# A list scheduler with clocks sets the order of attention and z1 on one Trainium2 core

## The chip, the core and the metric

The kernel runs on one core of a Trainium2 chip. The core has five engines with a queue each, which work through their queues in order: TensorE (PE, matmuls), VectorE (DVE), ScalarE (ACT), GpSimd (POOL) and SyncE (SP, which issues most DMAs). Matmul results land in PSUM, eight banks of 2 KB per partition. The metric is the device time of one execution in microseconds; the kernel before takes 1897.5 us (median of three runs, 1896.04 to 1898.21).

## What is computed

The input x is 2048 tokens of 576 features. With xn = layernorm(x), the reference computes, cut to what matters:

```
qkv = xn @ wqkv                                # 32 heads of 18
scores = q k^T * 18**-0.5, kept where 0 <= query - key < 256
s = softmax(scores) @ v @ wo
z = gelu(x @ w_in);  z1, z2 = z[:, :2304], layernorm(z[:, 2304:])
g = w_sp @ z2 + b_sp                           # w_sp is 2048 x 2048
out = x + s * silu((z1 * g) @ w_out)
```

The softmax subtracts each row's maximum, so scores are computed twice: once to find the maxima (rows are queries), once, transposed, for the exponential.

## The kernel before

Matrix products of the projections run with operands split in a high and a low half (fp32r), three matmuls for one. The stages stand one after the other: q and k projection (to 145 us), v, the z2 half of the gelu (204 to 442 us), **attention together with z1** (to 915 us), the product with w_sp by seven half-size products (to about 1600 us), and the output products.

In z2 and z1, PE is used as two row groups: contraction rows 0 to 63 and 64 to 127 hold different weights, and matmuls of the two groups run side by side. Class `RowGroups` hands out the matmuls of a 512-token tile: `lower()` issues the next one of the lower group (L288), `upper()` of the upper (L306). A tile has 13 or 14 on each side. A tile's upper side may start only when the lower side is through, which a one-element copy on VectorE (`turn`, L291) marks; then the tile is copied out by ScalarE (`evict`, L536). z1 has 72 tiles in three PSUM banks (pool `mmp`); its 972 matmuls per group are the filler for attention.

Attention handles 16 units: four heads, half of the queries. Head j of a unit lies in the lower row group for even j and in the upper for odd j. Per unit there are:

- 32 **row maxima** (`row_max`): a matmul of 256 or 384 columns into a bank of pool `sps` (L585 in the lower group, L589 in the upper, output `sp`), reduced by VectorE into `mx` (L478). After 32 of them `mx` is spread out, transposed in two matmuls (L490), split in two pieces by VectorE (L494, L495) and put beside q by four GpSimd DMAs (`put_max`, L498), so that the score matmul itself subtracts the maximum. One unit makes 35 items of a generator: 32 maxima, the spread, a pause, and both transposes.
- 32 or 40 **scores** (`scores`): a matmul into a bank of pool `tps` (also L585 or L589, output `tps`) and an exponential by ScalarE into `pt` (L627). Blocks on the edge of the band are masked by GpSimd (L630, L633).
- **PV** (`pv`): fp32 matmuls of all 128 rows by 32 columns per head (L647), whose result ScalarE copies out (L657) and SP stores.

The order is that of the program text, since the scheduler of the framework is switched off here. `beside` sets each score or maximum next to one z1 matmul of the other row group. In the main loop each score is followed by up to `FILL` = 2 pairs of z1 matmuls, as many as the shares `WEIGHT` allow, and up to three maxima at the rate `RMN` = 35 per unit, `FIRST` = 53 ahead. PV comes in bursts when three (unit, key block) entries are ready. `clock` is a rough time that only delays stores and puts (`after`, `tick`). Each of `sps` and `tps` has two banks, used in turn, and `ops` one. In z2, 53 items of the stream of maxima are issued in the last 26 tiles, two a tile, beside z2's matmuls.

Of the kernel before, what the change touches and what calls it, by code (L numbers as in the profile page):

```python
# [10 lines left out]
F32 = mybir.dt.float32  # L11
# [29 lines left out]
RMN = 35  # L41
LEAD = 18
FIRST = RMN + LEAD
SUMS_AT = 112
NPT = 6
FILL = 2
LAG = 8
ZORDER = [8 * (i // 8) + i % 2 * 4 + i % 8 // 2 for i in range(16)]
NORM_AT = 2
GAP = 7  # L50
# [3 lines left out]
TAIL = 56  # L54
HEAD = 14
_SHARE = [18 + 0.4 * (i >= 8) for i in range(16)]
WEIGHT = [sum(_SHARE[:i + 1]) / sum(_SHARE) for i in range(16)]

# [11 lines left out]
def kernel(  # L70
# [181 lines left out]
    with ExitStack() as early:  # L252
# [15 lines left out]
        class RowGroups:  # L268

            def __init__(self, tiles):  # L270
                self.tiles, self.n, self.i = tiles, -1, 0
                self.low, self.up, self.ready, self.hooks = [], [], [], {}

            def lower(self):
                if self.i == len(self.low):
# [7 lines left out]
                    if self.n < 2:  # L283
                        hook()
                    else:
                        self.hooks[self.n] = hook
# [3 lines left out]
                if self.i == len(self.low):  # L290
                    dve.tensor_copy(turn, self.last[3][0:1, 0:1])  # L291
                    self.ready.append(self.last)
                return True
# [5 lines left out]
            def upper(self):  # L299
                if not self.up:  # L300
                    if not self.ready or not (self.over or self.n > self.ready[0][0] and self.i >= LAG):
                        return False
                    self.up = self.ready.pop(0)
                    self.up = [self.up[0], self.up[1], self.up[2]]
                m, up, done = self.up
                up.pop(0)()  # L306
                if not up:
                    self.up = []
                    done()
                    if m + 2 in self.hooks:  # L310
                        self.hooks.pop(m + 2)()
                return True

# [101 lines left out]
        with ExitStack() as ph:  # L415
# [45 lines left out]
            def row_max(u):  # L461
                g, half = UNITS[u]
                base = 0 if half == 0 else 6
                mx = aa.tile([P, 2, 2, 4, 8], F32, name="mx")
                for a in range(2):
                    for i in range(8):
                        qb = 8 * half + i
                        w = 384 if qb >= 2 else 256
                        k0 = (max(qb - 2, 0) - base) * P
                        m0 = {0: 256, 1: 128}.get(qb, 0)  # L470
                        for b in range(2):
                            j = 2 * a + b
                            ps = sps.tile([P, 384], F32, name="sp")
                            mm = partial(pe.matmul, ps[:, :w], q_of(u, j, DR)[:, i * P:(i + 1) * P],
                                         k_of(u, j, DR)[:, k0:k0 + w], start=True, stop=True)
                            beside((mm, None) if b == 0 else (None, mm))
                            junk = aa.tile([P, 384], mybir.dt.bfloat16, name="junk")
                            dve.tensor_tensor_reduce(out=junk[:, :w], in0=ps[:, :w], in1=band[:, m0:m0 + w],  # L478
                                                     scale=1.0, scalar=-3.0e38, op0=ALU.add, op1=ALU.max,
                                                     accum_out=mx[:, a, b, 0, i:i + 1])  # L480
                            yield
                dve.tensor_copy(mx[:, :, :, 1:], mx[:, :, :, 0:1].to_broadcast([P, 2, 2, 3, 8]))
                yield
                yield
                hi = aa.tile([P, P], F32R, name="mh")
                m = aa.tile([P, P], F32R, name="mhl")
                pts_ = [sps.tile([P, 384], F32, name="sp")[:, :64] for _ in range(2)]
                for n in range(2):
# [833 lines left out]
```

## Time and profile before

| | before |
|---|---|
| median of three runs | 1897.5 us |
| profiled execution, its time | 1899.3 us |
| profiled execution, its span | 1897.6 us |
| PE busy | 1861.4 us (98%) |
| VectorE busy | 1075.8 us (57%) |
| ScalarE busy | 885.9 us (47%) |
| GpSimd busy | 297.7 us (16%) |
| granted TensorE clock | 0.999 |
| stage of z2 | 204 to 442 us |
| stage of attention and z1 | 438 to 915 us |

The span runs from the first instruction to the last; the execution's time has a little around it. Busy time is the union of an engine's records, so PE counts as busy when one of the two row groups is. A record of a matmul covers its whole latency; how often matmuls follow each other has to be read from starts.

### The profile page before, as it was taken

Reading aid. Unit: us, or ns where it says so; the run is one execution under the profiler, and the core shown is the slowest. Engines: PE = TensorE matmul, PEld = TensorE weight load, DVE = VectorE, ACT = ScalarE, POOL = GpSimd, SP = SyncE. Lnnn points to the kernel's source line nnn. Section 1 sums busy time; section 2 is a strip of 40 time slices with the busy share of each in tenths; the row PEclk is TensorE's granted clock in tenths of the full one; section 3 lists DMA queues with packets and bytes.
Section 4 is the critical chain, followed back from the end, with each engine's and each line's share of the span. In section 5 each row is a group of like instructions: output and inputs, shape, how many; then the busy total and the mean of one; then the engine's idle time right before and its main releaser. Section 6 shows DMA issues by size and latency. Waiting matters only on the chain.

```text
span 1897.6 us, 35556 instructions
## 1 busy us (share of the span) xinstructions
PE 1861.4 (98%) x13296; PEld 1584.7 (84%) x13296; DVE 1075.8 (57%) x2496; ACT 885.9 (47%) x1663; POOL 297.7 (16%) x419
## 2 busy tenths in 40 slices
PE   6999999999999999999999999999999999999998
PEld 5889999997677767666888888888888888999998
DVE  6521233367677776662386767676776877533222
ACT  3222222225666666667565565545655454432221
POOL 1002243343433443434000000000000000000000
PEclk9999999999999999999999999999999999999999
DMA  7664589964565665554676686757868578855442
GB/s 229 185 167 137 181 277 277 298 234 132 142 149 144 156 157 143 142 130 133 230 241 203 219 290 216 232 165 254 274 222 304 189 261 264 296 167 162 137 140 67
DMA packets 221383, 376.98 MB, mean 199 GB/s; under 512 B 41306, under 2 KB 118234, under 8 KB 221082
## 3 DMA queue, kind: packets, MB, share of 16 engines
q1 hardware_dynamic: 216378, 367.49, 62.7%
q10 hardware_dynamic: 2304, 5.09, 0.7%
q0 software_dynamic: 2528, 2.13, 0.4%
q8 instruction: 105, 1.72, 0.4%
q14 instruction: 68, 0.56, 0.1%
HBM read 256.52 MB, written 117.55 MB: 197 GB/s over the span
## 4 chain that ended last, share of the span: by engine, by line
PE 90%; DMA 5%; ACT 2%; DVE 2%; issue 1%; SPq 1%; POOL 0%; ACTq 0%; POOLq 0%
PE acc L1095 36%; PE po L1245 12%; PE mm L288 12%; PE mm L306 8%; PE mm L391 6%; PE ops L647 4%; PE vps L548 3%; PE tps L585 3%; PE sp L585 2%; PE wops L1199 2%; DMA s_d<-so 1%; PE sp L589 1%; DMA z_d<-zt 1%; PE tps L589 1%; ACT pt L627 1%
## 5 line engine op out<-in xcount | busy, mean ns | idle before, releaser
L1095 PE MATMUL acc<-sph,zh 128*128 128x512 f32 x1008 | 392.4, 389 | 0.2 <-DVE u L1068 0.2
L1095 PE MATMUL acc<-sph,zl 128*128 128x512 f32 x1008 | 392.3, 389 | 0.0
L1095 PE MATMUL acc<-spl,zh 128*128 128x512 f32 x1008 | 392.2, 389 | 0.0
L478 DVE CUSTOM_DVE_ANT_0 junk<-sp,band 128x384 bf16<-128x384 f32 (+1 forms) x512 | 265.6, 537 | 101.3 <-PE sp L585 32.9
L627 ACT ACTIVATE pt<-tps 128x384 f32<-128x384 f32 (+2 forms) x576 | 241.0, 439 | 107.3 <-PE tps L585 56.5
L306 PE MATMUL mm<-b,z1wh 64*128 64x512 f32 x648 | 237.7, 413 | 0.7 <-DVE turn L291 0.7
L235 DVE TENSOR_TENSOR spl<-spr,sph 128x1024 fp32r<-128x1024 f32 x166 | 203.2, 1224 | 50.2 <-ACT sph L235 47.0
L288 PE MATMUL mm<-b,z1wh 64*128 64x512 f32 x648 | 224.0, 395 | 0.0
L1095 PEld LDWEIGHTS acc<-sph,zh 128*128 128x128 f32 x1008 | 189.3, 188 | 40.0 <-issue 0.9
L1095 PEld LDWEIGHTS acc<-spl,zh 128*128 128x128 f32 x1008 | 189.3, 188 | 39.3
L1095 PEld LDWEIGHTS acc<-sph,zl 128*128 128x128 f32 x1008 | 189.3, 188 | 39.3
L235 ACT ACTIVATE zh<-b 128x384 fp32r<-128x384 f32 x144 | 75.6, 525 | 244.3 <-PE acc L1095 244.0
L288 PE MATMUL mm<-z2wh,b 64*128 64x384 f32 x720 | 185.5, 333 | 2.6 <-ACT zt L805 2.6
L306 PE MATMUL mm<-z2wh,b 64*128 64x384 f32 x720 | 183.6, 333 | 0.4 <-DVE turn L291 0.4
L235 ACT ACTIVATE sph<-spr 128x1024 fp32r<-128x1024 f32 x166 | 174.0, 1048 | 3.8 <-DMA spr<-in_w_sp_dram 2.7
L1245 PE MATMUL po<-b,yh 128*128 128x288 f32 x896 | 157.3, 296 | 0.5 <-ACT gs L1259 0.5
L235 DVE TENSOR_TENSOR zl<-b,zh 128x384 fp32r<-128x384 f32 x144 | 80.1, 557 | 116.0 <-ACT zh L235 115.8
L306 PE MATMUL mm<-b,z1wl 64*128 64x512 f32 x324 | 133.5, 412 | 0.0
L1245 PEld LDWEIGHTS po<-b,yh 128*128 128x128 f32 x896 | 132.7, 189 | 0.7 <-ACT gs L1259 0.7
L288 PEld LDWEIGHTS mm<-z2wh,b 64*128 64x128 f32 x720 | 128.4, 184 | 3.6 <-ACT zt L805 3.4
L805 ACT ACTIVATE zt<-mm 128x384 f32<-128x384 f32 x96 | 47.2, 491 | 176.3 <-PE mm L306 99.2
L306 PEld LDWEIGHTS mm<-z2wh,b 64*128 64x128 f32 x720 | 128.6, 184 | 1.0 <-DVE turn L291 1.0
(172 smaller groups left out, 3925.5 us busy)
## 6 DMA issues: line engine op xcount, KB each, us to landing
spr<-sc_d SPq DMA_DIRECT2D x96, 512.0 KB
spr<-in_w_sp_dram SPq DMA_DIRECT2D x72, 512.0 KB
zr<-z_d SPq DMA_DIRECT2D x136, 192.0 KB
st_d<-qkhl SPq DMA_DIRECT2D x72, 256.0 KB
z_d<-zt SPq DMA_DIRECT2D x96, 192.0 KB
z_d<-z1o SPq DMA_DIRECT2D x72, 256.0 KB
z1t<-z_d SPq DMA_DIRECT2D x72, 256.0 KB
yr<-y_d SPq DMA_DIRECT2D x48, 384.0 KB
```

The costliest lines, as they stand in the source:

```text
L235: job()
L288: self.low[self.i]()
L306: up.pop(0)()
L391: pe.matmul(ps, w, r, start=n == 0, stop=n == len(pl) - 1)
L478: dve.tensor_tensor_reduce(out=junk[:, :w], in0=ps[:, :w], in1=band[:, m0:m0 + w], scale=1.0, scalar=-3.0e38, op0=ALU.add, op1=ALU.max, ac ...
L548: pe.matmul(ps[:, i, :288], r, w[:, i * 288:(i + 1) * 288], start=n == 0, stop=n == len(pl) - 1)
L585: pair[0]()
L627: act.activation(pt[:, j, d0:d0 + n * P], ps[:, (qa - a) * P:(qa - a + n) * P], AF.Exp, scale=scale)
L647: pe.matmul(o_ps[c][32 * j:32 * j + 32, (lo - 4 * c) * P:(hi - 4 * c + 1) * P], vgs[u][:, kb - k0, j * VW:j * VW + 32], pt[:, j, (lo - kb) ...
L805: act.activation(zv, ps[:, :ZW], AF.Gelu_apprx_tanh)
L1095: pe.matmul(acc[j], z[:, ps], w[:, cs], start=s == i == 0 and n in OPENS, stop=s == 7 and i == 2, skip_group_check=True)
L1245: pe.matmul(po[i][:, a, :288], y[:, i * P:(i + 1) * P], w[:, a * 288:(a + 1) * 288], start=f == 0 and m == 0, stop=f == NF - 1 and m == 2)
```

## The change

`beside`, the shares and `FILL`, `LEAD`, `HEAD`, `TAIL` and `GAP` are gone. Class `Plan` keeps clocks: `tg[g]` (when each row group is free), `last` (start of the last matmul in the queue), `td`, `ta`, `tp` (VectorE, ScalarE, GpSimd), `free[k]` (when each of four score banks can be written), `ops` (the PV bank), and for z1's banks `banks` and `turned`. `step()` looks at the row group that is free first and issues the first thing that the clocks allow: a PV burst, a row maximum or its transposes, a score, a z1 matmul; if nothing fits, the group's clock moves on by 20 ns. The two pools of two score banks become four pools of one bank, which maxima and scores share; the one that is free first is taken. Bursts want `BURST` = 4 entries instead of 3, z1's lag between the row groups is 0 instead of 8, and the transposes of a unit are two separate items, one per row group. Evictions and stores are issued by the planner's clock too. During z2, `FIRST` = 84 items (now 34 per unit) are issued in the last 42 tiles.

```diff
-RMN = 35
-LEAD = 18
-FIRST = RMN + LEAD
+FIRST = 84
...
+BURST = 4
+LATE = 40
+AHEAD = 900
...
+            banks = []
+
+            def score_bank():
+                banks.append(banks.pop(0))
+                return banks[-1].tile([P, 384], F32, name="sp")
...
-            def beside(pair):
-
-                was = z.n
-                if pair[0]:
-                    pair[0]()
-                    count(was, z.upper())
-                else:
-                    count(was, z.lower())
-                    pair[1]()
-                spend(86)
...
+                def room(self, t, until):
+                    k = min(range(4), key=self.free.__getitem__)
+                    if self.free[k] > t or until - t > AHEAD:
+                        return False
+                    self.bank = self.free.pop(k)
+                    self.free.append(self.bank)
+                    banks.insert(0, banks.pop(k))
+                    return True
+
+                def begin(self, g, ns, bank=0):
+                    self.start = max(self.tg[g], self.last, bank)
+                    self.last = self.start
+                    self.tg[g] = self.start + ns
+
+                def pass_of(self, g):
+                    t = max(self.tg[g], self.last)
+                    m = z.next_upper() if g else z.next_lower()
+                    if m == -1:
+                        return False
+                    if m is not None:
+                        if g and (not z.over and z.n <= m or self.turned.get(m, 0) > t):
+                            return False
+                        if not g and (z.over or self.banks.get(m - 3, 9e9) > t):
+                            return False
+                    self.begin(g, MM)
+                    return z.upper() if g else z.lower()
+
+                def row_max(self, g):
+                    t = max(self.tg[g], self.last) + LATE
...
+                    u = next((u for u in maxima[:2 - len(turning)] if u.left[g]), None)
+                    if not u or self.loaded.get((u.u, 2 * u.left[g][0][0] + g), 9e9) > t or not self.room(t, self.td):
+                        return False
+                    w = u.width(g)
+                    self.begin(g, 0.417 * w + 13, self.bank)
+                    u.take(g)
+                    self.td = max(self.td, self.start + 210 + 0.43 * w)
+                    self.free[-1] = self.td + 65 + 140 + 1.09 * w
+                    self.td += 170 + 1.04 * w
...
+                def score(self, g, u, s, js):
+                    kb, qa, qz = s
+                    t = max(self.tg[g], self.last) + LATE
+                    j = next((j for j in js if j % 2 == g), None)
+                    if j is None or self.maxed.get(u, 9e9) > t:
+                        return False
+                    if (u, kb) not in pts and len(ring) == NPT and ring[0] in pending or not self.room(t, self.ta):
+                        return False
+                    js.remove(j)
+                    n = qz - qa + 1
+                    w = max(n, 2) * P
+                    self.begin(g, 0.417 * w + 13, self.bank)
+                    self.ta = max(self.ta, self.start + 210 + 0.43 * w)
+                    self.free[-1] = self.ta + 53 + 170 + 0.84 * n * P
+                    self.ta += 50 + 0.835 * n * P
...
+                def burst(self):
...
+                    if not n or self.ops > t or n < BURST and todo[n - 1][2] != 4 * todo[0][1] + 3:
+                        return False
+                    t += 190
+                    for _ in range(n):
+                        e = todo.pop(0)
+                        t += {1: 210, 2: 415, 3: 626, 4: 836}[e[4] - e[3] + 1]
+                        if pv(*e):
+                            self.ta = max(self.ta, t + 300) + 493
+                            self.ops = self.ta + 170
+                    self.last = t
+                    self.tg = [t + 96] * 2
+                    return True
...
+                def step(self, *item):
+                    nonlocal clock
+                    g = int(self.tg[1] < self.tg[0])
+                    clock = max(self.tg[g], self.last)
+                    tick()
+                    if self.burst():
+                        return
+                    self.more()
+                    if self.row_max(g):
+                        return
+                    if item and self.score(g, *item):
+                        return
+                    if not self.pass_of(g):
+                        self.pass_of(1 - g)
+                        self.tg[g] = max(self.tg[g] + 20, self.last)
...
-                sps = open_pool(ph, "sps", bufs=2, space=PSUM)
+                banks += [open_pool(ph, name, space=PSUM) for name in ("sp0", "sp1")]
...
-                        next(stream)
+                        early_max(FIRST - due_max)
...
-                tps = open_pool(work, "tps", bufs=2, space=PSUM)
+                banks += [open_pool(work, name, space=PSUM) for name in ("sp2", "sp3")]
...
-                        scores(u, *s, j)
...
+                        plan.until_scored(u, s, js, 3 - j)
```

In the changed kernel's lines, L284 and L303 are z1's (and z2's) lower and upper matmuls, L487 a row maximum, L619 a score and L641 PV; `sp` is the score bank's tile, whichever of the four.

PE's queue behind a PV burst in the middle of the stage; `tps` is a score's output, `sp` a maximum's, `mm` a z1 tile; before:

```order
L585 MATMUL tps_11313<-att4_1776 128x256
L306 MATMUL mm_11056<-b0_97,z1wl_10768 128x512
L288 MATMUL mm_11318<-b0_97,z1wh_10767 128x512
L589 MATMUL sp_11317<-att2_1198 128x384
L288 MATMUL mm_11318<-b3_100,z1wh_10767 128x512
L589 MATMUL tps_11323<-att4_1776 128x256
L288 MATMUL mm_11318<-b0_97,z1wl_10768 128x512
L306 MATMUL mm_11056<-b1_98,z1wh_10767 128x512
L585 MATMUL sp_11329<-att2_1198 128x384
L306 MATMUL mm_11056<-b4_101,z1wh_10767 128x512
L585 MATMUL tps_11334<-att5_5608 128x256
```

Behind a burst at about the same place after:

```order
L487 MATMUL sp_11471<-att3_1778 128x384
L303 MATMUL mm_11170<-b2_99,z1wl_10608 128x512
L487 MATMUL sp_11476<-att3_1778 128x384
L303 MATMUL mm_11170<-b5_102,z1wh_10607 128x512
L619 MATMUL sp_11481<-att5_5747 128x256
L619 MATMUL sp_11486<-att4_1779 128x256
L284 MATMUL mm_11420<-b1_98,z1wh_10997 128x512
L303 MATMUL mm_11170<-b5_102,z1wl_10608 128x512
L284 MATMUL mm_11420<-b4_101,z1wh_10997 128x512
L303 MATMUL mm_11306<-b0_97,z1wh_10997 128x512
L284 MATMUL mm_11420<-b1_98,z1wl_10998 128x512
```

Before, every score and every maximum has one or two z1 matmuls of the other group between it and the next; after, several stand together where banks are free, and z1 matmuls stand together where none is.

PE's queue in z2's 56th tile of 96 (`mm` is a z2 tile); before:

```order
L288 MATMUL mm_3814<-z2wl_2996,b0_97 128x384
L306 MATMUL mm_3740<-z2wh_2995,b2_99 128x384
L288 MATMUL mm_3814<-z2wh_2995,b0_97 128x384
L306 MATMUL mm_3740<-z2wh_2995,b4_101 128x384
L288 MATMUL mm_3814<-z2wh_2995,b3_100 128x384
L306 MATMUL mm_3740<-z2wl_2996,b2_99 128x384
```

The same place after:

```order
L284 MATMUL mm_3817<-z2wl_2999,b0_97 128x384
L303 MATMUL mm_3743<-z2wh_2998,b2_99 128x384
L284 MATMUL mm_3817<-z2wh_2998,b0_97 128x384
L303 MATMUL mm_3743<-z2wh_2998,b4_101 128x384
L487 MATMUL sp_3827<-att0_1196 128x256
L303 MATMUL mm_3743<-z2wl_2999,b2_99 128x384
L284 MATMUL mm_3817<-z2wh_2998,b3_100 128x384
```

The first maximum now stands here, beside a z2 matmul of the upper group; before, the first one stands 16 tiles later.

## Rows read from the trace of the kernel before

**Rows 1.** The stretches: us, busy (instructions) of PE, PEld, DVE, ACT, POOL; PEclk; DMA; GB/s.

```profile
378.00:416.00 38.00, 38.00 (x441) 37.81 (x439) 26.20 (x95) 7.99 (x16) 15.93 (x12) 1.00 0.69 234
447.00:900.00 453.00, 441.48 (x4264) 315.21 (x4266) 295.59 (x1128) 300.76 (x730) 183.64 (x300) 1.00 0.55 143
```

**Rows 2.** Instructions of tile mm, z1's lines: count, min/median/max ns, first and last start.

```profile
L288 PE MATMUL mm<-b,z1wh x648: 383/392/502, 437.8 to 909.7; 64*128 64x512 f32 x162
...
L288 PE MATMUL mm<-b,z1wl x324: 383/392/502, 438.3 to 909.4; 64*128 64x512 f32 x162
...
L306 PE MATMUL mm<-b,z1wl x324: 383/393/502, 442.9 to 914.9; 64*128 64x512 f32 x162
```

**Rows 3.** The stretches, of L288 alone, then of L585 alone: PE, PEld, clock, DMA.

```profile
206.00:240.00 34.00, 34.00 (x198) 34.00 (x197) 1.00 0.69 223
378.00:416.00 38.00, 37.80 (x206) 35.46 (x205) 1.00 0.69 234
901.00:909.00 8.00, 8.00 (x37) 6.30 (x36) 1.00 0.73 173
...
378.00:416.00 38.00, 4.83 (x15) 2.65 (x15) 1.00 0.69 234
```

**Rows 4.** Groups by shape, PE, 447 to 900 us: count, busy us, mean ns, idle.

```profile
L585 PE MATMUL sp<-att 54*128 54x384 f32 x206 | 77.4, 376 | 2.5 <-DVE mhl L495 1.3 <-DVE mx L478 0.2
...
L585 PE MATMUL tps<-att 56*128 56x384 f32 x192 | 75.3, 392 | 3.0 <-ACT pt L627 2.0
...
L647 PE MATMUL ops<-pt,vg 128*32 128x384 f32 x512 | 52.4, 492 | 0.0
L647 PE MATMUL ops<-pt,vg 128*32 128x256 f32 x448 | 34.4, 379 | 0.0
L585 PE MATMUL tps<-att 56*128 56x256 f32 x96 | 31.2, 325 | 1.1 <-ACT pt L627 1.0
...
L647 PE MATMUL ops<-pt,vg 128*32 128x128 f32 x448 | 23.3, 280 | 0.0
L585 PE MATMUL sp<-att 54*128 54x256 f32 x25 | 8.0, 320 | 3.7 <-DVE mhl L495 3.7
```

**Rows 5.** The chain that ended last, 447 to 915 us: start, length, what.

```profile
458.48 1.86 PE ops L647 x24
...
473.93 1.44 PE ops L647 x24
```

**Rows 6.** PE in order of time round a burst: start, length, what.

```profile
500.31 0.33 PE L589 MATMUL sp<-att 54*128 54x384 f32 x1
500.57 1.50 PE L647 MATMUL ops<-pt,vg 128*32 128x384 f32 x24
502.00 0.44 PE L585 MATMUL tps<-att 56*128 56x384 f32 x1
```

**Rows 7.** The waits, 447 to 900 us: us in total, times, longest.

```profile
PEld tps L585 <- ACT pt L627: 24.8, 72, 0.8
...
PEld sp L585 <- DVE mx L478: 10.6, 40, 0.5
PEld sp L585 <- DVE mhl L495: 9.7, 14, 0.9
...
PEld tps L589 <- ACT pt L627: 7.5, 26, 0.8
```

**Rows 8.** PE and its weight loads in order of time, 507.7 to 509 us.

```profile
507.79 0.34 PE L585 MATMUL tps<-att 56*128 56x384 f32 x1
...
508.77 0.44 PE L585 MATMUL tps<-att 56*128 56x384 f32 x1
...
508.77 0.18 PEld L585 LDWEIGHTS tps<-att 56*128 56x128 f32 x1 [0.27 <-ACT pt L627]
508.77 0.18 PEld L306 LDWEIGHTS mm<-b,z1wh 64*128 64x128 f32 x1
```

**Rows 9.** The page's groups: busy us, mean ns, idle and what ended it.

```profile
L478 DVE CUSTOM_DVE_ANT_0 junk<-sp,band 128x384 bf16<-128x384 f32 (+1 forms) x512 | 265.6, 537 | 101.3 <-PE sp L585 32.9
```

More of the change, by code (lines that the diff above doesn't have):

```diff
@@ L459, in spend @@
                 tick()
[L461 to L488, printed above, removed]
-                    r = slice(64 * n, 64 * n + 64)
-                    pe.transpose(pts_[n], mx[r].rearrange("p a b n i -> p (a b n i)"), ident[r, r])
-                spend(60)
-                for n in range(2):
-                    r = slice(64 * n, 64 * n + 64)
-                    dve.tensor_scalar(hi[:, r], pts_[n], -1.0, None, ALU.mult)
-                    dve.scalar_tensor_tensor(m[:, r], f32(hi[:, r]), low, pts_[n], ALU.mult, ALU.subtract)
-                def put_max(n):
-                    pool.dma_start(f32(q_of(u, n)[DR:DS]), f32(m[32 * n:32 * n + 16, :]))
-                for n in range(4):
-                    after(2500 + 700 * n, partial(put_max, n))
-                yield
@@ L693, in finish @@
-                after(1500, store)
+                sp.dma_start(d_d[4 * g:4 * g + 4, cs], ou[DH::32, :])
+                for i in range(4):
+                    h = 4 * g + i
+                    sp.dma_start(o_d[h * DH:(h + 1) * DH, cs], ou[32 * i:32 * i + DH, :])
+                    d0 = max(512 - h * DH, 0)
+                    if d0 < DH:
+                        sp.dma_start(o_d[64 + h * DH + d0:64 + (h + 1) * DH, cs], ou[32 * i + d0:32 * i + DH, :])
+            stores, prep, plan_at = [], [], [0]
@@ L770 @@
                 z2_out = []
-                stream = (step for u in range(NU) for step in row_max(u))
+                maxima, turning = [Maxima(u) for u in range(NU)], []
                 def z2_tiles():
@@ L818, with early_max @@
                 z = RowGroups(chain(z2_tiles(), z1_tiles()))
+                def early_max(n):
+                    if turning and turning[0].turns[0]:
+                        turning[0].turn(0)
+                    elif turning:
+                        u = turning.pop(0)
+                        u.turn(1)
+                        for n in range(4):
+                            after(2500 + 700 * n, partial(u.put, n))
+                    else:
+                        u, b = maxima[0], n % 2
+                        if b:
+                            z.lower()
+                        u.take(b)
+                        if not b:
+                            z.upper()
+                        if not u.left[1]:
+                            turning.append(maxima.pop(0))
+                            u.spread()
+                    spend(86)
                 while (z.n, z.i) < (6 * NS + 1, LAG + 1):
@@ L893 @@
+                        plan.until_scored(u, s, js, 3 - j)
                         if t == 12 and u + 1 < NU:
                             load_v(u + 1)
[L895 to L897 removed]
+                assert not maxima and not turning
+                while todo:
+                    plan.step()
                 while prep:
[L899 to L902 removed]
+                    plan.step()
@@ L903 @@
                 while extras:
                     extra(1)
-                fill(9)
+                while stores:
+                    plan.step()
                 work.close()
@@ L908 @@
                 load_w(2)
-                while z.lower():
-                    count(z.n, 1 + z.upper())
+                while not z.over:
+                    plan.step()
                 split_step(2)
```

232 lines of the change are left out of this document (148 added, 84 removed).

## The prediction, made before the result was known

> **What bounds the kernel now.** I read four views, in this order. First the table of stretches: between 447 and 900 us PE is busy 441.5 of 453.0 us at clock 1.00, while VectorE is busy 295.6 us, ScalarE 300.8 us, GpSimd 183.6 us and the DMA engines 55% [rows 1]. Taken alone that row says PE-bound. It counts PE as busy when either row group runs, though; the stage runs two 64-row groups side by side, so the second view is needed: how much work each group has. The stage begins with the first lower-group matmul of z1 at 437.8 us and ends with the last upper-group one, which starts at 914.9 us and is through its columns at 915.1 [rows 2]: 477.3 us.
>
> Work of one group, from counts times spacing. A 512-column z1 matmul follows its predecessor in its group after 0.227 us (37 records touch the 8.00 us from 901 to 909; (8.00+0.39)/37), a 384-column one after 0.173 us ((34+0.33)/198) [rows 3]; on the line through both, 256 columns take 0.119 us. Either group has 648+324 = 972 z1 matmuls [rows 2]: 220.6 us. Row maxima: 206 of 384 and 25 of 256 columns per group, 38.6 us; scores: 192 and 96, 44.6 us [rows 4]. By the order the upper group also ends the last z2 tile here, 22 matmuls, 3.8 us. Together 307.6 us for the longer group. Counted along the queue from one PV burst to the next, 3.5 us go where one group runs out of work before the other.
>
> PV uses the whole array, so both groups stop. A burst of 8 blocks of 128 columns takes 1.86 us, one of 6 takes 1.44 us [rows 5]: 0.215 us a block. The 448, 448 and 512 records of one, two and three blocks are eight to a block row (four heads, two records each) [rows 4], so 56 + 112 + 192 = 360 blocks, 77.4 us. Round a burst of 6, the last maximum before it, started at 500.31 us, is through its columns at 500.48, and the score behind it starts at 502.00, its record 0.44 us where 0.34 is usual [rows 6]: 1.62 us for 1.29 us of columns. I take 0.3 us a burst: 64 bursts, 19.2 us.
>
> So 477.3 - 307.6 - 3.5 - 77.4 - 19.2 = **69.6 us of the stage are waits in PE's queue**. The third view, the waits, names them: weight loads of scores wait 24.8 and 7.5 us for ScalarE's exponential, those of row maxima 10.6 us (lower group) for VectorE's maximum and 9.7 us for the two operations behind a transpose [rows 7]. All are waits for a score bank, two for maxima and two for scores. The fourth view shows what one costs: a score starts at 507.79 us; the next one in that bank has its weight load at 508.77, 0.98 us later, and the upper group's load, which needs nothing, starts at the same instant; the score's record is 0.44 us, its predecessor's 0.34, so its columns begin some 0.10 us after the load [rows 8]. A bank can thus be used again **1.08 us** after its last use if ScalarE is free, and whoever asks sooner stops both groups.
>
> [...]
>
> **The change, part by part.** *Same work.* No matmul, exponential or maximum is added or dropped; 30 of the 512 maxima and two transposes move, and the order changes.
>
> *More maxima during z2.* 31 more items (84 for 53). In z2 a maximum simply takes a slot: from 378 to 416 us the lower group ran 206 z2 matmuls and 15 maxima [rows 3], 221 in 38.33 us, the same 0.173 us as without them. Two groups share, so 31 x 0.087 = **+2.7 us** in z2. VectorE is busy 26.2 of those 38 us [rows 1], so it hides its side; if not, an item costs its 0.54 us [rows 9] and 31 cost 17 us, the upper end; nothing in these rows would make it a gain. The put DMAs of unit 1 now stand in GpSimd's queue ahead of the last combos; the first score is later than both, so nothing is charged. On SyncE's queue the loads of a unit's heads stay at the same four items two units ahead, some 50 us in a stage of 16 units; stores that wait for an eviction stand ahead of them in both versions, and the DMA engines, at 55%, go to about 60% when the same bytes move in 430 us. In the stage each group keeps 195 maxima of 384 and 22 of 256 columns by the order, 36.3 us: the longer group's work falls to 305.3 us.
>
> *Fewer bursts.* A burst now wants four blocks of keys ready instead of three; in the order there are 56 bursts for 64: 56 x 0.3 = 16.8 us, **-2.4 us**.
>
> *Order between bursts.* Counted as above, the uneven ends now make 8.2 us for 3.5: **+4.7 us**, since scores and maxima no longer alternate strictly between the groups.
>
> *Waits.* This is the main term. Along either order I added the spacings above from one use of a bank to the next. Before, the median is 0.52 us, and 943 of 1,069 re-uses come sooner than 1.08 us (0.92 for 256 columns); they are short by 501 us together, of which 69.6 us were lost, because one wait lengthens the distance of all four banks. After, with four banks shared and each given when the planner thinks it free, the median is 1.26 us, 263 of 1,034 are too soon, short by 30 us together. The lower end is the old ratio, 30 x 69.6/501 = 4.2 us. The count leaves out items that find another ahead of them on VectorE (65% busy) or ScalarE (66%) [rows 1], so I take **22 us**, nearer to the whole 30 us. No gain at all (69.6), or worse, belongs to the rivals.
>
> *Sum.* Stage after: 305.3 + 8.2 + 77.4 + 16.8 + 22 = 429.7 us, against 477.3: -47.6. With z2's +2.7: -44.9 us. The profiled execution took 1899.3 us (span 1897.6), so 1854.4; the median of the runs is 1.8 us below that execution: **1853 us**. Nothing behind the stage changes: the next stage's first tiles are prepared during the last unit in both versions, in the order z1 still has 25 lower and 46 upper matmuls left after the last score (55 and 78 before), about 10 us in which PV's stores drain and the third weight tile is loaded; if that load is late, the next stage starts late by what is missing of some 5 us.
>
> **Rivals.** *Just in time is too late* (slower). The planner calls a bank free at the time of the load, not of the columns: for a 384-column score it counts 0.92 us in all, against 0.98 to the load and 1.08 to the columns [rows 8]. If each re-use is placed at exactly that time, each stops PE by some 0.11 us or more: 1,034 x 0.11 = 114 us of waits in place of 69.6, stage 521.7 us, kernel 1,945 us. It decides from (69.6 - 2.7)/0.11 = 608 re-uses that wait in full. Against it: 771 of 1,034 have PE work of more than 1.08 us between them, and each wait gives the other three banks the same 0.11 us.
>
> *Half of it comes back* (still faster). VectorE's queue paces the maxima, so that a bank is held by a maximum behind two others, and a score of the other kind now waits for VectorE too, which it never did with banks of its own. Waits of 47 us: 1,878 us. For it: the shared banks; against: both engines are at two thirds.
>
> *PE is full* (hardly faster). If the 97% of the row were the bound, at most 453.0 - 441.5 = 11.5 us could be had [rows 1]; less z2's 2.7, 8.8 us: 1,889 us (the three terms of work in the stage cancel). Against it is the count per group.
>
> *The planner does not do what it says.* Were z1 spent early, the last units would run without filler. In the order every unit from 2 to 15 keeps 43 to 69 matmuls of z1 per group, so I give this next to nothing.
>
> **How the numbers follow.** Forecast (waits 8 to 35 us) 0.64; half comes back 0.19; too late 0.08; PE is full 0.06; other 0.03. Its own range is 1838 to 1867. To hold 8 in 10 it must reach into the half case: 1836 to 1883. This kernel's measurement tells 0.2% (4 us) from no change: faster 0.88, same 0.04, slower 0.08.
>
> **What would show it.** In the changed profile: the z1 stage of about 430 us; z2 longer by about 3 us; the weight-load waits for ScalarE and VectorE together below some 25 us (52.6 us in the four rows now); VectorE and ScalarE busy some 70% of the stage with the same busy time; 56 bursts. If the stage is short but the kernel is not, look at the first tiles of the next stage. Wrong: waits for scores on VectorE of tens of us (half), or nearly every score's load behind a release with 0.1 us each (too late).

## The result, and the profile after

The changed kernel took 1868.05 us (median of four executions, 1864.91 to 1875.19) beside 1897.86 us for the kernel before: a ratio of 0.9848, 95% interval 0.9816 to 0.9881. Measured a second time, later and beside other kernels, it was 0.9866 (0.9852 to 0.9879). The forecast was 1853 us, 45 us faster; 25 to 30 us came. The direction and the main mechanism held, and a third of the gain or more is missing. The time lies 1 us above the forecast's own range (1838 to 1867) and inside the wider one, which holds because it reaches into the "half" case. (One execution of the run one_clock below took 4,665 us for some 1,875; it is the one that was profiled, so that run's time is that of the other three, and it has no stage.)

The stage is counted as in the prediction, from the first z1 matmul. Three rows give its ends: the last matmul of z1 and the first one of the product with w_sp (L1239), which is the next thing TensorE does. Columns are count, min/median/max ns, first and last start.

```profile
L284 PE MATMUL mm<-b,z1wh x648: 383/392/625, 437.2 to 880.9; 64*128 64x512 f32 x162
L303 PE MATMUL mm<-b,z1wl x324: 383/392/625, 442.3 to 885.9; 64*128 64x512 f32 x162
L1239 PE MATMUL acc<-sph,zh x1008: 389/389/497, 886.2 to 1571.6; 128*128 128x512 f32 x168
```

The stage fell from 477.3 us [rows 2] to 886.2 - 437.2 = 449.0 us, by 28.3 us. The forecast said 429.7. The w_sp product behind it takes 686.2 us in both. (The output products took 225.9 us in this one execution and 231.2 to 231.3 us in the kernel before and in every other profile quoted below, so the whole times are compared by their ratios, and stages by profile.)

The stretches, with the columns of [rows 1]; the last three lines are of the stage's start.

```profile
378.00:416.00 38.00, 38.00 (x440) 37.82 (x438) 26.14 (x96) 8.05 (x17) 17.59 (x15) 1.00 0.65 220
447.00:880.00 433.00, 422.87 (x4300) 318.25 (x4301) 268.06 (x1066) 285.60 (x730) 181.93 (x296) 1.00 0.58 149
...
447.00:452.00 5.00, 4.57 (x41) 4.14 (x41) 0.14 (x1) 4.92 (x14) 2.64 (x5) 1.00 0.86 180
452.00:457.00 5.00, 3.55 (x20) 2.84 (x19) 2.16 (x9) 2.87 (x8) 2.27 (x4) 0.76 0.90 227
457.00:462.00 5.00, 5.00 (x55) 3.05 (x55) 2.87 (x12) 2.15 (x6) 0.23 (x1) 0.90 0.17 55
```

PE is as "busy" as before, 97.7% for 97.5%, in a stage that is 28 us shorter: the row did not bound the stage, as the prediction held. What TensorE waits for does tell the two kernels apart. The waits from 447 to 880 us (total us, times, longest); row maxima are L487 and scores L619, both with output `sp` now, since the banks are shared, so that a maximum can wait for an exponential and a score for VectorE:

```profile
PEld mm L284 <- DVE z1wl L535: 8.7, 12, 1.3
PEld sp L487 <- ACT pt L621: 5.4, 18, 1.2
PEld sp L487 <- DVE mx L490: 5.3, 21, 1.0
...
PEld sp L619 <- ACT pt L621: 3.2, 17, 0.2
PEld sp L619 <- DVE mx L490: 3.1, 12, 0.7
ACT z1wh L579 <- DMA z1raw<-in_w_z_dram: 2.7, 2, 1.7
...
PE sp L487 <- DMA att<-st_d: 1.6, 2, 1.5
...
PEld mm L284 <- ACT z1wh L535: 1.3, 1, 1.3
PEld sp L619 <- DVE mhl L506: 1.2, 4, 0.7
```

[rows 7] leaves out one row of bank waits of the kernel before, that of the upper group's maxima:

```profile
PEld sp L589 <- DVE mx L478: 7.5, 32, 0.6
```

The reader should see two things. The bank waits, 24.8 + 10.6 + 9.7 + 7.5 in [rows 7] and these 7.5, together 60.1 us, are 5.4 + 5.3 + 3.2 + 3.1 + 1.2 = 18.2 us. (They are waits of weight loads, some of which pass while earlier matmuls run: PE as a whole is idle for 10.1 of the 433.0 us. The view lists only waits over 0.15 us. Shorter ones of the same kinds, counted in the two traces, are 129 with 11.0 us before and 191 with 15.0 us after.) And the first row is new: z1's own matmuls wait 8.7 + 1.3 = 10.0 us for their weights to be split into high and low halves. The kernel before has no row in which a z1 matmul waits for them. One such wait, VectorE in order of time:

```profile
604.25 0.56 DVE L490 CUSTOM_DVE_ANT_0 junk<-sp,band 128x384 bf16<-128x384 f32 x1 [0.63 <-PE sp L487]
604.74 0.08 DVE L490 DVE_READ_ACCUMULATOR2_ANT mx<- 128x1 f32 x1
604.74 0.14 DVE L287 COPY turn<-mm 1x1 f32<-1x1 f32 x1
604.81 0.54 DVE L490 CUSTOM_DVE_ANT_0 junk<-sp,band 128x384 bf16<-128x384 f32 x1
605.28 0.07 DVE L490 DVE_READ_ACCUMULATOR2_ANT mx<- 128x1 f32 x1
605.28 0.94 DVE L535 TENSOR_TENSOR z1wl<-z1raw,z1wh 128x256 fp32r<-128x256 f32 x3
```

and the weight load that needs it:

```profile
605.74 0.18 PEld L284 LDWEIGHTS mm<-b,z1wl 64*128 64x128 f32 x1 [1.01 <-DVE z1wl L535]
```

VectorE was even idle for 0.63 us at 603.6; the three subtractions simply stood behind two more maxima in its queue. L535 is the line that issues whatever part of the split is left when a tile's first matmul is due. It should have nothing left: `more()` issues the six jobs ahead of time, but only while the planner's clock of the engine is at most 200 ns ahead of PE, and it rarely is: of the 51 subtractions in this trace L535 issues 50, of ScalarE's 51 copies 10. Nor does the planner know of the weights when it picks a z1 matmul.

By the prediction's own subtraction, 449.0 - 305.3 - 8.2 - 77.4 - 16.8 = 41.3 us of the stage are still waits where 22 were forecast: 18.2 for banks and 10.0 for z1's weights by the rows, and 13.1 that these rows do not name, among them the gap in the stretch 452 to 457 and the short waits.

### The profile page after: what moved, and what is told of

It reads as the page before. It is cut to its first block, busy times and chain, and to the rows that moved or that the text cites. A ratio compares the mean times of both kernels' runs of the same rounds, so it can differ in the third digit from the quotient of the medians.

```text
span 1863.2 us, 35869 instructions
## 1 busy us (share of the span) xinstructions
PE 1830.6 (98%) x13296; PEld 1577.6 (85%) x13296; DVE 1063.2 (57%) x2496; ACT 869.7 (47%) x1663; POOL 298.3 (16%) x419
## 4 chain that ended last, share of the span: by engine, by line
PE 92%; DMA 3%; DVE 2%; issue 1%; ACT 1%; SPq 0%; POOL 0%; ACTq 0%; DVEq 0%
PE acc L1239 37%; PE po L1389 12%; PE mm L303 12%; PE mm L284 11%; PE mm L396 6%; PE ops L641 4%; PE vps L561 3%; PE sp L487 3%; PE sp L619 2%; PE wops L1343 2%; DMA att<-st_d 1%; DMA s_d<-so 1%; DMA xr<-in_x_dram 0%; PE tpt L378 0%; DVE z1wl L535 0%
## 5 line engine op out<-in xcount | busy, mean ns | idle before, releaser
L1239 PE MATMUL acc<-sph,zh 128*128 128x512 f32 x1008 | 392.3, 389 | 0.2 <-DVE u L1212 0.2
L1239 PE MATMUL acc<-sph,zl 128*128 128x512 f32 x1008 | 392.2, 389 | 0.0
L1239 PE MATMUL acc<-spl,zh 128*128 128x512 f32 x1008 | 392.1, 389 | 0.0
L490 DVE CUSTOM_DVE_ANT_0 junk<-sp,band 128x384 bf16<-128x384 f32 (+1 forms) x512 | 259.1, 535 | 113.1 <-PE sp L487 67.4
L621 ACT ACTIVATE pt<-sp 128x384 f32<-128x384 f32 (+2 forms) x576 | 224.1, 450 | 104.6 <-PE sp L619 81.1
L284 PE MATMUL mm<-b,z1wh 64*128 64x512 f32 x648 | 226.5, 396 | 1.3 <-ACT z1wh L535 0.9
L303 PE MATMUL mm<-b,z1wh 64*128 64x512 f32 x648 | 226.9, 400 | 0.0
L1239 PEld LDWEIGHTS acc<-sph,zh 128*128 128x128 f32 x1008 | 189.2, 188 | 40.1 <-issue 0.9
L1239 PEld LDWEIGHTS acc<-spl,zh 128*128 128x128 f32 x1008 | 189.2, 188 | 39.4
L1239 PEld LDWEIGHTS acc<-sph,zl 128*128 128x128 f32 x1008 | 189.2, 188 | 39.3
L284 PE MATMUL mm<-z2wh,b 64*128 64x384 f32 x720 | 188.8, 332 | 0.0
L303 PE MATMUL mm<-z2wh,b 64*128 64x384 f32 x720 | 183.4, 333 | 0.4 <-DVE turn L287 0.4
L487 PE MATMUL sp<-att 54*128 54x384 f32 (+1 forms) x512 | 165.3, 359 | 3.7 <-DMA att<-st_d 1.6
L619 PE MATMUL sp<-att 56*128 56x384 f32 (+1 forms) x576 | 167.1, 342 | 0.6 <-DVE mhl L506 0.3
L284 PE MATMUL mm<-b,z1wl 64*128 64x512 f32 x324 | 129.1, 399 | 4.5 <-DVE z1wl L535 4.2
```

The source lines that it names most:

```text
L284: self.low[self.i]()
L487: pe.matmul(ps[:, :w], q_of(self.u, j, DR)[:, i * P:(i + 1) * P], k_of(self.u, j, DR)[:, k0:k0 + w], start=True, stop=True)
L619: mm()
L621: act.activation(pt[:, j, d0:d0 + n * P], ps[:, (qa - a) * P:(qa - a + n) * P], AF.Exp, scale=scale)
L1239: pe.matmul(acc[j], z[:, ps], w[:, cs], start=s == i == 0 and n in OPENS, stop=s == 7 and i == 2, skip_group_check=True)
```

## The experiments

Ratios are to the kernel before, run on the same chip in the same hours. The stage runs from the first z1 matmul to the first w_sp matmul.

| run | ratio (95%) | stage us | w_sp us |
|---|---|---|---|
| before | 1 | 477.4 | 686.2 |
| changed | 0.9848 (0.9816 to 0.9881) | 449.0 | 686.2 |
| changed_again | 0.9866 (0.9852 to 0.9879) | 449.2 | 686.2 |
| z1_weights_early | 0.9868 (0.9843 to 0.9893) | 444.7 | 686.3 |
| head_load_margin | 0.9819 (0.9796 to 0.9841) | 442.7 | 686.2 |
| bank_margin | 0.9882 (0.9859 to 0.9905) | 445.5 | 693.4 |
| two_and_two_banks | 0.9892 (0.9852 to 0.9933) | 453.3 | 691.7 |
| raw_and_weights_early | 0.9801 (0.9787 to 0.9816) | 437.7 | 686.2 |
| both_causes_and_margin | 0.9798 (0.9784 to 0.9813) | 435.1 | 686.9 |
| no_further_lead | 0.9837 (0.9822 to 0.9851) | 446.8 | 686.2 |
| before_with_further_lead | 1.1283 (1.1263 to 1.1303) | 721.4 | 686.2 |
| one_clock | 0.9866 (0.9851 to 0.9881) | - | - |
| both_causes_no_further_lead | 0.9848 (0.9834 to 0.9862) | 443.4 | 692.6 |
| both_causes_less_late | 0.9790 (0.9777 to 0.9803) | 432.5 | 690.6 |

### Are z1's weights worth their 10 us?

```
-    if j < 3 and self.ta <= self.last + 200:
+    if j < 3 and self.ta <= self.last + 900:
-    elif j >= 3 and self.td <= self.last + 200 and self.ta <= self.last + 600:
+    elif j >= 3 and self.td <= self.last + 900 and self.ta <= self.last + 600:
```

> The changed kernel, but the split of z1's next weights is put in the queues as soon as VectorE or ScalarE has less than 0.9 us of planned work ahead instead of 0.2 us. Theory (the planner holds the split back until an engine is free, and z1's matmuls then wait for their weights): the 13 waits for z1wl, 8.9 us, and the one for z1wh, 1.3 us, go; the kernel is 8 to 10 us faster than the changed one, about 1859 us. Rival (what is missing of the gain is bank waits, and a VectorE that takes the split earlier delays a maximum instead): the waits for z1wl go but those for score banks grow by as much, and the time stays within 3 us of the changed kernel.

The waits for z1's weights went, the stage fell by 4.3 us only, and the whole time did not improve, as the rival had it. The waits of this run, 447 to 880 us, name the taker, which is not VectorE, as the rival thought:

```profile
PEld sp L487 <- ACT pt L621: 11.0, 27, 2.8
ACT z1wh L579 <- DMA z1raw<-in_w_z_dram: 7.2, 4, 2.2
PEld sp L619 <- ACT pt L621: 6.6, 25, 1.0
```

ScalarE now meets the first copy of a split before the raw weights have landed, waits for that DMA up to 2.2 us, and every exponential queued behind it waits too; a maximum then waits for a bank that an exponential has still to read, and PE stops all the same:

```profile
645.80 0.42 ACT L579 ACTIVATE z1wh<-z1raw 128x256 fp32r<-128x256 f32 x1 [2.23 <-DMA z1raw<-in_w_z_dram]
...
646.54 0.18 PEld L487 LDWEIGHTS sp<-att 54*128 54x128 f32 x1 [2.79 <-ACT pt L621]
```

So the DMA has to start sooner as well. The next run keeps this edit and issues the DMA one z1 tile (some 6 us) earlier:

```
+    if f + 1 < FH // P and c == 0:
+        raw = fetch_z1(f + 1)          # the DMA alone
     if f + 1 < FH // P and c == 1:
-        nxt = load_z1(f + 1)
+        nxt = load_z1(f + 1, raw)      # tiles and split jobs
```

> The changed kernel with the z1 weight splits let out early, as in z1_weights_early, and with the DMA of the raw z1 weights started one z1 tile sooner, so that ScalarE's part of the split no longer waits for it. Theory that the 10.2 us which TensorE waits for z1 weights are a cost of their own: with both causes of the delay gone the stage from the first z1 product to the w_sp products is 439 to 441 us against 449.0 of the changed kernel, with at most 2 us of z1-weight waits and about 13 us of waits for exponentials as in the changed kernel. Rival, that this time is slack that any other wait takes over: z1-weight waits near 0, but waits for exponentials at 20 us or more and a stage of 444 to 448 us.

Stage 437.7 us, 11.3 less than the changed kernel: the first theory, and a little more than it. The waits for exponentials are 6.9 + 4.6 = 11.5 us, for 17.6 in the run above and 8.6 in the changed kernel. No z1 matmul waits for its weights; one maximum waits 0.6 us behind the split:

```profile
PEld sp L487 <- ACT pt L626: 6.9, 31, 0.4
PEld sp L624 <- ACT pt L626: 4.6, 22, 0.3
PEld sp L487 <- DVE mx L490: 3.6, 19, 0.3
PE sp L487 <- DMA z_d<-z1o: 1.8, 1, 1.8
PEld sp L624 <- DVE mx L490: 1.4, 7, 0.3
...
PEld sp L487 <- DVE z1wl L584: 0.6, 1, 0.6
```

### The gap at the stage's start

In the changed kernel the first maxima of the stage wait for their heads' q and k (PE in order of time):

```profile
452.48 0.39 PE L303 MATMUL mm<-b,z1wh 64*128 64x512 f32 x1
454.33 0.35 PE L487 MATMUL sp<-att 54*128 54x256 f32 x1 [1.45 <-DMA att<-st_d]
```

With the lead of 84 items the stage begins with the maxima of unit 2, and two of this unit's four heads are loaded only at the first and third score. The planner takes a load to have landed after 9 us. SyncE issues the DMAs of these two heads from 446.1 to 451.4 us, and the last had not landed when the maximum's turn came. Here the planner is told 16 us, in unit 0 alone:

```
-    plan.loaded[heads_at[t]] = clock + 9000
+    plan.loaded[heads_at[t]] = clock + (16000 if u == 0 else 9000)
```

> The changed kernel, but during the first unit the planner counts 16 us instead of 9 us until a head's load has landed. Theory (a maximum of unit 2 stands in the queue before its head has landed at 452.7 us; PE waits 1.6 us for the DMA, and the granted clock then falls to 0.50 for some 4 us): no wait for the load, clock 1.00 from 447 to 500 us, 3 to 5 us faster than the changed kernel. Rival (the dip of the clock comes of something else, or the maxima that are put off are missed later): the dip stays, or the time stays within 2 us.

Stage 442.7 us, 6.3 less, with the gap gone and the clock at 1.00 throughout the start:

```profile
452.00:457.00 5.00, 5.00 (x42) 4.44 (x38) 1.24 (x4) 4.66 (x14) 3.19 (x6) 1.00 0.84 199
457.00:462.00 5.00, 5.00 (x61) 3.50 (x59) 0.69 (x4) 3.46 (x9) 1.96 (x5) 1.00 0.74 224
```

That is more than the 1.6 us of the wait. What the rest is was not settled: the lower clock is one candidate (see the last section), the different order (55 bursts) another.

Both causes together (with the planner's present moved along in its preparing loop besides):

> The same, with the 16,000-cycle margin for the first heads' loads of head_load_margin besides, and with the planner's own notion of the present moved along in its preparing loop. Theory that the missing 15 us of the forecast are the z1-weight waits (10 us) and the late head load with the clock drop behind it (4 to 6 us): stage 433 to 437 us against 449.0, the whole program 1853 to 1858 us, ratio to the kernel before 0.976 to 0.980. Rival, that the two overlap, or that the stage is bound by TensorE's own instructions and uneven ends: stage 440 to 444 us, whole program 1861 to 1866 us.

Stage 435.1 us, 13.9 less: inside the first theory's 433 to 437. The two edits had given 11.3 and 6.3 alone, 17.6 together, so some 4 us overlap, as the rival had it. The whole time is 1860.9 us, ratio 0.9798, inside the first theory's ratio; in microseconds it is 3 above it. Beside raw_and_weights_early (0.9801) the whole time gains nothing measurable: in these two profiles the stage is 2.6 us shorter and z2 1.9 us longer (236.7 for 234.8). PE is busy 422.0 of 423.0 us, and bank waits are 6.2 + 4.5 + 4.3 + 1.9 = 16.9 us:

```profile
447.00:870.00 423.00, 422.01 (x4321) 322.62 (x4319) 271.69 (x1074) 287.79 (x733) 181.79 (x296) 1.00 0.59 155
```

### Would later use of a bank cost or save?

The rival "just in time is too late" said that a bank is reused 0.1 us too soon each time. This run makes the planner wait 110 ns longer:

```
-LATE = 40
+LATE = -70
```

(and moves the planner's present along as above).

> The changed kernel, but the planner uses a score bank only when it is planned free 70 ns before the group is free, instead of up to 40 ns after: 0.11 us later, which is what lies between a weight load and its columns. Theory (bank waits are some 20 us and most of it is this 0.1 us): the waits for ScalarE's exponential, VectorE's maxima and the pieces of the transposes fall from 20.4 to below 10 us, and since z1 fills in, the kernel is 5 to 10 us faster. Rival (the planner's clock is off by more than that, in both directions): the waits stay above 15 us and the time within 3 us; also possible is a loss, when z1 is spent early and the last units run without it.

Bank waits fell to 4.4 us (2.1 + 1.2 + 0.7 + 0.4 in four rows), and nothing was gained. Where an item is not allowed yet, a z1 matmul goes in its place, and z1 was spent at 861.5 us, while the last PV matmuls ended at 882 us; the w_sp product began at 883.6 us and ran with gaps itself. Its stretches, the second at that end:

```profile
457.00:462.00 5.00, 4.81 (x40) 2.03 (x40) 1.52 (x5) 1.13 (x4) 0.00 (x0) 0.66 0.38 116
880.00:900.00 20.00, 15.09 (x68) 10.72 (x61) 8.10 (x9) 8.73 (x12) 0.00 (x0) 0.84 0.50 147
```

A milder form, on top of both_causes_and_margin, has `LATE = 0`:

> both_causes_and_margin with the planner's allowance for a bank that comes free late set from 40 ns to 0, so that it waits a little longer before it uses a bank again. Theory that the 19.2 us of waits left for banks come from uses placed right at the modelled time: they fall by 4 to 8 us, while z1 products fill in and the stage is 430 to 434 us. Rival, that z1 is then spent before the last unit as in bank_margin: waits fall, but the w_sp products start no earlier than at present, stage 434 to 440 us.

The theory held for the stage, 432.5 us, and for the waits, which fell from 16.9 to 3.2 + 2.5 + 1.9 + 0.5 = 8.1 us. What the rival feared came as well: z1 ends at 866.3 us, 8 us before the stage does, and the w_sp product took 3.7 us longer. The two balance: the ratio is 0.9790 beside 0.9798, inside either interval. Here fewer waits no longer buy time, since the filler runs out.

### What the further lead, the banks and the clocks bring

The lead, undone in the changed kernel:

```
-FIRST = 84
+FIRST = 52
...
-    self.loaded, self.maxed, self.ready = {divmod(n, 4): t for n in range(10)}, {0: t, 1: t + 4000}, {}
+    self.loaded, self.maxed, self.ready = {divmod(n, 4): t for n in range(10)}, {0: t}, {}
```

(The second edit belongs to the first: the maxima of unit 1 are then not all done when the stage starts.)

> The changed kernel with 52 row-maxima items ahead of z1, as many as the kernel before has, in place of 84; the list scheduler, the row-group clocks and the shared banks stay. By the forecast the 32 items cost z2 2.7 us and take that and a little more from the stage: z2 about 1 to 3 us shorter, stage 450 to 454 us against 449.0, whole program within 4 us of the changed kernel. Rival, that the further lead is what makes the banks' waits fall: waits for banks of 30 us or more against 20.4, stage of 460 us or more, whole program 1878 or later.

As the forecast had it for z2 and the whole: z2 is 231.9 us for 234.1 (231.4 for 234.1 without PE's waits for ScalarE's copies: 2.7 us), the waits for banks are 7.2 + 4.8 + 3.2 + 2.6 = 17.8 us, no different, and the whole time is within 0.1 to 0.3% of the changed kernel. The stage is 2 us shorter where 1 to 5 us longer was expected: PE has no wait for a head's load here, since the maxima of unit 2 come later. The lead is not what makes the banks free. The opposite edit, a longer lead in the kernel before, was meant to confirm it:

```
-LEAD = 18
+LEAD = 35
```

> The kernel before with its row maxima run 35 units of its lead ahead in place of 18, so that more of them fall into z2, and nothing else changed. By the forecast the order and the banks bring the gain, and the lead alone moves work: within 4 us of the kernel before. Rival, that the lead brings a good part of it: 10 us or more faster than the kernel before, with the waits for the banks clearly under their 62.6 us.

It shows something else. With 17 items more (70 for 53) the maxima stand in the queue before the loads of their heads have landed, and PE waits for them 47 times:

```profile
563.67 0.39 PE L306 MATMUL mm<-b,z1wl 64*128 64x512 f32 x1
568.38 0.55 PE L585 MATMUL sp<-att 54*128 54x256 f32 x1 [4.31 <-DMA att<-st_d]
```

and in the waits of the stage, 447 to 1150 us:

```profile
PE sp L589 <- DMA att<-st_d: 84.0, 25, 4.7
PE sp L585 <- DMA att<-st_d: 79.8, 22, 5.8
```

Both theories missed by 240 us, and the run says nothing on the lead; the lead of the kernel before is tied to its load points.

Two banks for maxima and two for scores, with the new scheduler:

```
-    k = min(range(4), key=self.free.__getitem__)
+    k = min((k for k in range(4) if self.kinds[k] == kind), key=self.free.__getitem__)
```

> The changed kernel, but two of the four score banks serve maxima alone and two serve scores alone, as before the change; planner, bursts and maxima during z2 stay. Theory (the gain comes from an order that does not ask for a bank before it is free, and sharing adds to it because the engine that is behind gets more banks): slower than the changed kernel by 5 to 15 us, still faster than before. Rival (the clocks alone make the gain and sharing nothing): within 3 us of the changed kernel. Rival (sharing couples the two engines and costs): faster than the changed kernel by over 3 us.

```profile
PEld sp L619 <- ACT pt L621: 12.0, 44, 2.0
PEld sp L487 <- DVE mx L490: 9.6, 33, 1.0
```

The two rows of waits are 21.6 us, where the four rows of the changed kernel for exponentials and maxima have 17.0 and the same kinds before 24.8 + 7.5 + 10.6 + 7.5 = 50.4. Sharing is worth 4 to 5 us of waits and at most 4.3 us of stage: this run's clock was also at 0.50 for 6.8 us near the stage's start, the changed kernel's for 3.4. Its w_sp product took 5.5 us longer, and its whole time, 0.9892, has an interval that reaches into the changed kernel's. The greater part of the fall comes with separate banks.

One clock for both row groups in the scheduler, which then alternates between them:

```
-    self.tg[g] = self.start + ns
+    self.tg = [self.start + ns / 2] * 2
+    self.side = 1 - g
```

> The changed kernel with a single clock for both row groups in its list scheduler: each item moves that clock by half its duration and the groups take strict turns. Shared banks, lead, margins and burst rule stay. By the forecast the row-group clocks decide only how even the two groups come out and how well the planned re-use of a bank meets the engines: uneven ends and bank waits together 5 to 15 us more than in the changed kernel, stage 454 to 464 us. Rival, that the clocks per row group are what makes the order fit: bank waits back to 47 us or more, stage 475 us or longer, no gain over the kernel before. Second rival, that they do nothing: stage 446 to 451 us.

Three executions took 1872.3 to 1877.1 us, the changed kernel beside it 1871.5 to 1876.2: in the whole time the second rival, the clocks per group do nothing that can be measured. Its stage and its waits are not known.

> The changed kernel as it is, run beside the three that follow, so that their stages and times are compared on one chip. Both theories: stage from the first z1 product to the w_sp products 448 to 450 us, ratio to the kernel before 0.982 to 0.988.

This is the control for these runs; its stage was 449.2 us.

Last, the faster version without the lead:

> both_causes_and_margin with 52 row-maxima items ahead of z1 in place of 84. By the forecast's price of 0.087 us an item z2 is 2.7 us shorter and the stage, which then keeps 32 more items, 2.8 us longer: stage 437 to 439 us against 435.1, whole program within 2 us of both_causes_and_margin. Rival, that the lead also saves waits in the stage: stage 442 us or more and the whole program 4 us or more slower than both_causes_and_margin.

0.5% (some 10 us) slower than with it, as the rival's numbers say, but not by waits in the stage, which the rival named: the bank waits are 7.0 + 5.2 + 3.5 + 1.8 = 17.5 us, as with the lead. z1 is spent at 870.2 us, and from there the attention's tail stands alone (PE in order of time):

```profile
870.17 0.39 PE L303 MATMUL mm<-b,z1wl 64*128 64x512 f32 x1
870.18 0.90 PE L624 MATMUL sp<-att 56*128 56x384 f32 x4
871.67 3.60 PE L624 MATMUL sp<-att 56*128 56x384 f32 x10 [0.59 <-ACT pt L626]
875.20 4.91 PE L646 MATMUL ops<-pt,vg 128*32 128x128 f32 x48
880.04 0.50 PE L1245 MATMUL acc<-sph,zh 128*128 128x512 f32 x1
```

Ten scores take 3.6 us, at the pace of ScalarE, whose exponentials follow each other there (14 in 4.45 us from 871.14), and the clock is 0.66 on average between 870 and 880 us. Then the operands of the w_sp product, split by the same ScalarE, are late too:

```profile
PE acc L1245 <- ACT sph L229: 3.6, 1, 3.6
```

## Why the prediction was right and where it was wrong

**What bounds the stage: right.** The prediction held that 97% of busy PE is no bound for two row groups; the rival "PE is full" held that it is. The changed stage is 28 us shorter at the same share, that of both_causes_and_margin 42 us at 99.8%, where that rival allowed 11.5 us.

**Bank waits: right, and somewhat too hopeful.** The forecast let 69.6 us shrink to 22. The rows went from 60.1 to 18.2 us, below the "some 25 us" that it named as the sign, and fell by 41.9 us where the sum took off 47.6. (Its "52.6 us in the four rows" leaves a fifth row out.) With the waits too short for the view they went from 71.1 to 33.2 us, by 37.9. Either way this is the main term, and it came 6 to 10 us short. Whether the short waits cost PE time was not shown.

**z1's weights: left out.** This is the step that failed: a term of 10.0 us, in no part of the sum and in no rival, and so put at nothing. It asked what the new order does to the score banks and not what it does to the other work queued on the same two engines. The split jobs were in the trace of before, and `more()` was in the diff with its condition; that maxima run ahead on VectorE by up to the 900 ns in the planner was the sign that the condition would fail. raw_and_weights_early gives the price in the stage: 11.3 us.

**The heads' loads: wrong for the first unit.** "Some 50 us" ahead is not what it has, since the stage starts with the maxima of unit 2. Elsewhere PE hardly waits for a load (1.6 us in all, 1.5 of them here). The mended kernels give a price of 2.6 us (behind the weights) to 6.3 us (alone).

**z2: right.** 233.6 us became 234.1, but the kernel before had 2.6 us in z2 in which PE waited for ScalarE's copies, the changed one none: 231.0 and 234.1, +3.1 for the forecast's +2.7. Those waits come and go between executions: changed_again has 3.1 us of them in a z2 of 238.1 us, which is 235.0 without, +4.0.

**Bursts, uneven ends, group work.** 56 bursts were there. The runs don't resolve these terms of 2 to 5 us one by one. One sign did not come: VectorE and ScalarE are busy 62% and 66% of the stretch, not some 70%, as both were busy for less time than before (268.1 for 295.6 us, 285.6 for 300.8, in stretches of 433 and 453 us); some 16 us of VectorE's are the 30 maxima that z2 now has.

**The rivals.** *Just in time is too late* fell by its time: the stage is 449.0 us, not 521.7. What it describes is there in small. 72 weight loads waited for a bank in the five rows and 191 more by less than 0.15 us, but the latter come to 15.0 us, not 114; and bank_margin, which removed most of the long waits and some 6 us of the short ones, gained nothing. *Half of it comes back* gave about the right time (1,878 us) by a mechanism that isn't there: bank waits are 18 us in the rows (33 with the short ones), not 47, and scores wait 3.1 us for VectorE, not tens. *The planner does not do what it says* got next to no chance since z1 lasts to the last unit in this order; that was right of this kernel, but three small edits (bank_margin, both_causes_less_late, both_causes_no_further_lead) ran into just that.

**The sum.** -47.6 us was forecast for the stage, all of it waits since the other terms cancel, and -28.3 came. By the rows, banks gave 41.9, z1's weights took 10.0 back, and 3.6 more went to waits that the rows do not name (9.5 us before, 13.1 after), the late load among them. With both causes mended the stage is 435.1 us, 5.4 us above the forecast. What these 5.4 us are was not settled: bank waits are 16.9 us there by the rows, under the 22 forecast, and 33.9 with the short ones.

Of what the change consists of, the shared banks bring some 4 us at most and the clocks per row group nothing measurable in the whole time; the lead brings nothing measurable in the changed kernel and 0.5% in the mended one. That leaves the placing of each score and maximum at a planned time for its bank. This is by elimination: it was not taken out by itself, and neither were the larger bursts, the lag of 0 in z1 or the planned evictions.

## What to carry to other kernels

When an order is rewritten so that one kind of wait goes, list everything else that queues on the engines that were waited for, with the time at which each is due, and ask whether the new planner knows of it: here 10 of 45 us went to jobs that it treated as filler for idle moments. Set a subtraction's remainder against every row of waits and not only the longest, and ask which waits are too short for the view: here four rows named 52.6 of 69.6 us, five 60.1, and with the short waits it was 71.1. And where one kind of work fills all gaps, its end is a deadline: bank_margin waited less, spent its filler 22 us early and gained nothing.

## What the runs showed of the hardware

In these runs stops of PE of 1.45 to 1.77 us were followed by a lower granted clock in some cases and not in others. After the gap of 1.45 us in the changed kernel it fell from 1.00 to 0.50 for 3.4 us, from about 454.6 to 458.0 us; changed_again had a gap of 1.71 us for the same load at 458.8 us, and the clock stayed at 1.00:

```profile
457.00:462.00 5.00, 2.94 (x22) 1.83 (x21) 2.62 (x10) 2.93 (x8) 1.71 (x3) 1.00 0.85 229
```

The two stages are 449.0 and 449.2 us, so the drop cost nothing that shows in the stage's length; but PE was idle for longer there in changed_again (1.71 and then 0.70 us), which may hide a cost. raw_and_weights_early kept 1.00 after 1.77 us, bank_margin had its drop (0.66 in the stretch shown above) after one of 1.74 us. What decides was not tried.

In z1_weights_early what stood in ScalarE's queue behind a copy that waited for its DMA waited too: ScalarE's waits for the raw weights came to 7.2 us, 4.5 more than in the changed kernel, and the weight loads' waits for exponentials rose from 8.6 to 17.6 us.
